# Attention with random features and a two-layer MLP on one core: the work of the first four pairs of heads, the key sums and the order of the instructions are changed

## The chip, the core and the metric

The kernel runs on one core of a Trainium2 chip. The engines that appear below are TensorE (PE in the rows; PEld is its weight load), VectorE (DVE), ScalarE (ACT), GpSimd (POOL) and SyncE (SP, which issues nearly all DMAs). The metric is device time in microseconds (us).

## The reference

There are 8 batches of 8 heads, 576 positions each, with a head dimension of 64 and 128 random features (`omega`). All data are float32.

```python
def phi(x):                                   # x is q or k, scaled by 64 ** -0.25
    proj = einsum('bhsd,md->bhsm', x, omega)
    h = proj - sum(x * x, -1) / 2             # the sum of squares of each row
    return exp(h - max(h, -1)) / sqrt(128)

kv = einsum('bhsm,bhsd->bhmd', k_p, v)
z = sum(k_p, axis=2)                          # the key sums
num = einsum('bhsm,bhmd->bhsd', q_p, kv)
den = einsum('bhsm,bhm->bhs', q_p, z) + 1e-06 # the denominators
x = (num / den) laid out as 4608 tokens x 512
out = silu(x @ w_in) @ w_out                  # w_in 512 x 2048, w_out 2048 x 512
```

## The kernel before, in words

The 64 heads are worked on as 32 pairs (`NWIN`); four pairs make a batch's 512 columns of `x`. Rows of a pair are held in nine blocks of 128 positions (`NC`), the middle one (`MID`) split between the two heads. For each pair n the stages are: loads of the transposed rows (`raw`) and of the plain rows (`nat`); the squares (`square`, L479, ACT) and their sums (`square_sum`, L488, DVE); projections (`project` L496, `project_mid` L502, PE, float32); row maxima (`top`, L509 and L511, DVE) and the bias made of maximum and square sum (`shift`, L517, DVE, tiles nbk and nbq); exponentials (`expo`, L534, ACT) into hk and hq. From hk come the key sums: for the first eight pairs (`DIRECT`) by PE alone (`zsum_direct`, L569 and L571), afterwards by four steps of additions on POOL (`sums`, L554 to L559) whose result `es`, 128x256, is summed over partitions by one float32 matmul against ones (`zsum`, L563). The denominators (`denom`) are nine blocks of products with the key sums, read from PSUM, each a fused multiply and add-up on DVE (L580) with a read of the accumulator, and then a reciprocal (L585). POOL scales hq by it (`normal`, L610), PE turns hq (`turn`, L616), ACT copies it out (`en_copy`, L628). `kv` (L592), its copies (`kt_copy` L597, `kw_copy` L605) and one turn (`kv_turn`, L600) prepare the right-hand factor of the numerators (`numer`, L654), whose result becomes `x` (`x_high` on ACT L673, `x_low` on DVE L678).

Meanwhile the weights are read, converted (`exponent` L738, `word` L752 to L758 on DVE) and split into a high and a low fp32r part (`weight_high` L771, `weight_low` L775 on POOL). The MLP of the first three batches runs as plain matmuls in three fp32r passes of 128x512 (L829 and L1075); the rest runs in two groups of block products with fewer multiplications (L914, L1028). Its matmuls lie between those of the attention on the same PE queue.

Nobody writes the order by hand: each step is a unit of a planner (`Plan`), with an engine, a due time (`key`), what it needs, the buffers it takes (`RINGS`, `HOMES`) and a cost (`COST`). `Plan.run` simulates the engines, and each engine executes its steps in the order so found. The due times are moved about by a table of seeds (`SHIFTS`). An engine that waits for one instruction holds back all that stand behind it.

## Time and profile before

| | |
|---|---|
| median of 3 runs (lowest to highest) | 1011.54 us (1010.02 to 1013.14) |
| the profiled execution | 1012.55 us |
| its span in the trace | 1010.4 us |
| PE busy | 982.1 us, 97% of the span |
| DVE busy | 760.1 us, 75% |
| ACT busy | 632.2 us, 63% |
| POOL busy | 367.4 us, 36% |
| mean granted clock of PE | 0.995 |

The span is counted from the first to the last instruction of the trace; 2.15 us of the profiled execution's time lie outside it. Busy shares are averages over stages that differ: the first 115 us are attention and weights, then attention and MLP are mixed, and from about 830 us on there is MLP alone. Ends of matmuls are modelled, so costs on PE are best read as the distance from the start of one group to the start of the next.

### The profile page before, as it was taken

Reading aid. Unit: us, or ns where it says so; the run is one execution under the profiler, and the core shown is the slowest. Engines: PE = TensorE matmul, PEld = TensorE weight load, DVE = VectorE, ACT = ScalarE, POOL = GpSimd, SP = SyncE. Lnnn points to the kernel's source line nnn. Section 1 sums busy time; section 2 is a strip of 40 time slices with the busy share of each in tenths; the row PEclk is TensorE's granted clock in tenths of the full one; section 3 lists DMA queues with packets and bytes.
Section 4 is the critical chain, followed back from the end, with each engine's and each line's share of the span. In section 5 each row is a group of like instructions: output and inputs, shape, how many; then the busy total and the mean of one; then the engine's idle time right before and its main releaser. Section 6 shows DMA issues by size and latency. Waiting matters only on the chain.

```text
span 1010.4 us, 17322 instructions
## 1 busy us (share of the span) xinstructions
PE 982.1 (97%) x5770; PEld 787.0 (78%) x5770; DVE 760.1 (75%) x1898; ACT 632.2 (63%) x1235; POOL 367.4 (36%) x447
## 2 busy tenths in 40 slices
PE   8799999999999999999999999999999999999997
PEld 7577877877777777777888777878887878888886
DVE  6988899876777677796666899995448977546962
ACT  6777776677656866676777775664858454334541
POOL 1455555777776775544642024120110100000000
PEclk9899999999999999999999999999999999999999
DMA  9667777787876976748986658875455677655665
GB/s 359 230 195 265 238 256 230 220 288 243 267 258 196 299 251 205 231 151 276 330 277 235 214 196 268 253 220 200 164 171 178 222 246 256 194 188 191 195 211 153
DMA packets 107592, 232.94 MB, mean 231 GB/s; under 512 B 14704, under 2 KB 39408, under 8 KB 107504
## 3 DMA queue, kind: packets, MB, share of 16 engines
q1 hardware_dynamic: 107200, 231.52, 69.8%
q8 instruction: 46, 0.75, 0.3%
q10 hardware_dynamic: 304, 0.33, 0.1%
q14 instruction: 42, 0.34, 0.1%
HBM read 182.52 MB, written 49.28 MB: 229 GB/s over the span
## 4 chain that ended last, share of the span: by engine, by line
PE 75%; DVE 15%; ACT 5%; DMA 3%; issue 2%; POOL 1%; DVEq 0%; ACTq 0%; POOLq 0%
PE ps_acc L914 18%; PE ps_acc L1028 12%; PE ps_acc L1075 10%; PE ps_h L829 7%; PE ps_att L496 4%; DVE prod L580 3%; PE ps_fx L829 2%; PE ps_att L1028 2%; PE ps_att L914 2%; PE ps_fx L1028 2%; PE ps_h L1028 2%; PE ps_fx L914 2%; PE ps_att L592 1%; PE ps_h L914 1%; DVE w L1018 1%
## 5 line engine op out<-in xcount | busy, mean ns | idle before, releaser
L914 PE MATMUL ps_acc<-w,x 128*128 128x512 f32 x792 | 189.7, 394 | 0.1
L610 POOL TENSOR_TENSOR hq<-hq,rd 128x384 f32<-128x384 f32 x96 | 91.0, 973 | 245.4 <-DVE rd L585 240.4
L914 PEld LDWEIGHTS ps_acc<-w,x 128*128 128x128 f32 x792 | 146.7, 188 | 32.4 <-DVE w L723 0.5
L1075 PE MATMUL ps_acc<-wo,gh 128*128 128x512 f32 x384 | 124.4, 405 | 0.0
L829 PE MATMUL ps_h<-x,w 128*128 128x512 f32 x432 | 116.7, 404 | 2.7 <-ACT gf L968 2.0
L1028 PE MATMUL ps_acc<-w,x 128*128 128x512 f32 x456 | 115.3, 394 | 0.0
L1028 PEld LDWEIGHTS ps_acc<-w,x 128*128 128x128 f32 x456 | 84.7, 188 | 18.8 <-DVE w L1018 0.4
L829 PEld LDWEIGHTS ps_h<-x,w 128*128 128x128 f32 x432 | 78.2, 189 | 21.4 <-issue 2.4
L580 DVE CUSTOM_DVE_ANT_0 prod<-hq,ps_att 128x128 f32<-128x128 f32 (+1 forms) x230 | 65.8, 286 | 22.2 <-ACT kw L605 8.6
L1075 PEld LDWEIGHTS ps_acc<-wo,gh 128*128 128x128 f32 x384 | 67.9, 188 | 14.4
L1028 PE MATMUL ps_acc<-gh,x 128*128 128x512 f32 x208 | 74.4, 396 | 1.4 <-DMA x<-wt 1.4
L1075 PE MATMUL ps_acc<-wo,gl 128*128 128x512 f32 x192 | 75.4, 393 | 0.0
L972 DVE TENSOR_TENSOR gl<-gf,gh 128x512 fp32r<-128x512 f32 x48 | 38.5, 802 | 24.9 <-ACT gf L968 24.6
L554 POOL TENSOR_TENSOR t<-hk 128x256 f32<-128x256 f32 x48 | 38.4, 820 | 36.2 <-ACT hk L548 24.8
L1028 PEld LDWEIGHTS ps_acc<-gh,x 128*128 128x128 f32 x208 | 39.0, 188 | 10.7 <-issue 1.8
L1075 PEld LDWEIGHTS ps_acc<-wo,gl 128*128 128x128 f32 x192 | 36.0, 188 | 8.1
L1028 PE MATMUL ps_acc<-gl,x 128*128 128x512 f32 x104 | 40.7, 391 | 0.0
L479 ACT ACTIVATE nat<-nat 128x576 f32<-128x576 f32 x58 | 40.0, 694 | 0.3 <-DMA nat<-kn 0.3
L628 ACT COPY en<-ps_att 128x384 f32<-128x384 f32 x45 | 21.2, 488 | 29.6 <-PE ps_att L616 24.8
L511 DVE TENSOR_REDUCE smk<-ps_att 128x4 f32<-128x512 f32 x42 | 27.7, 681 | 14.1 <-PE ps_att L496 10.1
L534 ACT ACT_TABLE_LOAD x24 | 30.8, 1283 | 12.0 <-DVE nbk L517 7.3
L829 PE MATMUL ps_fx<-x,w 128*128 128x512 f32 x144 | 37.8, 396 | 0.0
(434 smaller groups left out, 2379.8 us busy)
## 6 DMA issues: line engine op xcount, KB each, us to landing
x<-ws SPq DMA_DIRECT2D x84, 512.0 KB, 4.2
x<-wt SPq DMA_DIRECT2D x48, 512.0 KB, 4.2
x<-wo_d SPq DMA_DIRECT2D x72, 256.0 KB, 3.2
wo<-wo_d SPq DMA_DIRECT2D x32, 512.0 KB, 4.3
rawk<-kT SPq DMA_DIRECT2D x30, 352.0 KB, 4.3
rawq<-qT SPq DMA_DIRECT2D x30, 352.0 KB, 4.9
v<-v SPq DMA_DIRECT2D x30, 320.0 KB, 4.7
nat<-kn SPq DMA_DIRECT2D x29, 288.0 KB, 4.3
```

The source lines that it names most:

```text
L479: nc.scalar.activation(nat, nat, AF.Square, scale=SCALE * 0.5**0.5)
L496: nc.tensor.matmul(ps[:, i * M : (i + 1) * M], raw[r, o : o + P], oms[r], start=True, stop=True)
L511: nc.vector.tensor_reduce(m[:, 5 * j : 5 * j + 4], ps.rearrange("p (c m) -> p c m", m=M), AX.X, ALU.max)
L534: nc.scalar.activation(h[:, c], ps[:, i * M : (i + 1) * M], AF.Exp, bias=nb[:, c : c + 1])
L554: nc.gpsimd.tensor_tensor(t[:, j], e[:, 5 * j : 5 * j + 2], e[:, 5 * j + 2 : 5 * j + 4], ALU.add)
L580: nc.vector.tensor_tensor_reduce(out=prod[r], in0=e[r, c], in1=z[r, j * M : (j + 1) * M], scale=1.0, scalar=GUARD, op0=ALU.mult, op1=ALU.a ...
L610: nc.gpsimd.tensor_tensor(e[:, c], e[:, c], rd[:, c].unsqueeze(2).broadcast_to([P, 3, M]), ALU.mult)
L829: nc.tensor.matmul(ph, w[:, i], x[:, j], start=k == 0 and n == 0, stop=k == NK - 1 and n == 2)
L914: nc.tensor.matmul(ph, ws[:, u, kk * P : (kk + 1) * P], o[:, x], start=i in (0, 1, 4) and kk == 0 and n == 0, stop=kk == 1 and n == 2, ski ...
L972: nc.vector.tensor_tensor(gl, T.pop(("gf", t, f)), T["gh", t, f].bitcast(F32), ALU.subtract)
L1028: nc.tensor.matmul(T["qb", p, chain][d], w[:, u, d * P : (d + 1) * P], x, start=i in (0, 1, 4) and s == 0 and n == 0, stop=s == NS - 1 and ...
L1075: nc.tensor.matmul(T["po", t][j], g[:, js], w, start=f == 0 and n == 0, stop=f == NF - 1 and n == 2)
```

## The change

For the first four pairs (`SHARE`) the squares are made by POOL instead of ACT (the scale then becomes a small extra instruction on DVE), and the denominators by a copy of the key sums from PSUM to SBUF on ACT, products on POOL (two of 128x512, two of 64x128), and on DVE one reduction of 128x9x128, one small addition and the reciprocal. From the ninth pair on, POOL splits the key sums into a high and a low fp32r part (two more instructions of 128x256), and PE sums them in two fp32r passes instead of one float32 matmul; from the tenth on the turn of kv is no longer behind the key sums but behind the second group of turns of hq. The load of omega is issued by SP as its first DMA, no longer by ACT. A seventh warm-up matmul is added. The scratch tiles `prod` and `es` go; `zp` comes, and the products use a buffer of ring `en`. Costs, constants, the way of choosing among ready steps, and the whole table of seeds are other ones, so that the order on every engine is new.

```diff
-WARM = 6
+SHARE = 4
+WARM = 7
-    45253, 12939, 63401, 47171, 48605, 47566, 42730, 5774, 83395, 62489, 16880, 27634, 67040, 8136, 46225,
+    82336, 88449, 46253, 47699, 57731, 212, 16446, 12734, 86717, 29045, 39768, 53214, 56989, 74460, 88726,
...
     def load_omega():
-        nc.scalar.dma_start(omr, om_in)
+        nc.sync.dma_start(omr, om_in)
...
     def square(n, who):
         nat = T["nat", n, who]
+        if n < SHARE:
+            nc.gpsimd.tensor_tensor(nat, nat, nat, ALU.mult)
+            return
         nc.scalar.activation(nat, nat, AF.Square, scale=SCALE * 0.5**0.5)
...
+        if n < SHARE:
+            s = T["sm", n, who][:, 1, :NC]
+            nc.vector.tensor_scalar(s, s, SCALE * SCALE * 0.5, None, ALU.mult)
...
+    def sums_high(n):
+        T["zp", n] = zp = new("zp", [P, 2, 2, M], F32R)
+        nc.gpsimd.tensor_copy(zp[:, 0], T["es", n])
+
+    def sums_low(n):
+        zp = T["zp", n]
+        nc.gpsimd.tensor_tensor(zp[:, 1], T.pop(("es", n)), zp[:, 0].bitcast(F32), ALU.subtract)
 
     def zsum(n, ps):
-        es = T.pop(("es", n))
-        nc.tensor.matmul(ps[:, : 2 * M], ones, es.rearrange("p j m -> p (j m)"), start=True, stop=True)
+        zp = T.pop(("zp", n)).rearrange("p two j m -> p two (j m)")
+        for i in range(2):
+            nc.tensor.matmul(ps[:, : 2 * M], ones_r, zp[:, i], start=not i, stop=bool(i))
         T["z", n] = ps
...
+    def z_copy(n):
+        z, T["zs", n] = T.pop(("z", n)), new("t", [P, 2, M])
+        nc.scalar.copy(T["zs", n].rearrange("p j m -> p (j m)"), z[:, : 2 * M])
+
+    def weighted(n):
+        e, z = T["h", n, "q"], T.pop(("zs", n))
+        T["ez", n] = ez = new("en", [P, NC, M])
+        for j in range(2):
+            c, r = slice(5 * j, 5 * j + 4), slice(j * D, (j + 1) * D)
+            nc.gpsimd.tensor_tensor(ez[:, c], e[:, c], z[:, j : j + 1].broadcast_to([P, 4, M]), ALU.mult)
+            nc.gpsimd.tensor_tensor(ez[r, MID], e[r, MID], z[r, j], ALU.mult)
+
     def denom(n):
+        if n < SHARE:
+            den = new("den", [P, NC])
+            nc.vector.tensor_reduce(den, T.pop(("ez", n)), AX.X, ALU.add)
+            nc.vector.tensor_scalar(den, den, GUARD, None, ALU.add)
+            T["rd", n] = rd = new("rd", [P, NC])
+            nc.vector.reciprocal(rd, den)
+            return
...
         T["t", n, g] = ps[:, off : off + 3 * P]
+        if n > DIRECT and g == 1:
+            kv_turn(n, ps, 3 * P)
...
-    def zsum_turn(n, ps):
-        zsum(n, ps)
-        kv_turn(n, ps, 2 * M)
```

On POOL, at the start of the program, there stood no work of the attention before the first pair's scaling of hq (`hq<-hq,rd`); `w_475` and the like are homes of MLP weights:

```order
L443 MEMSET sides 64x128 x2
L610 TENSOR_TENSOR hq<-hq,rd 128x384 x3
L771 CAST w_475<-w_445 128x512
L775 TENSOR_TENSOR w_475<-w_445,w_475 128x512
L610 TENSOR_TENSOR hq<-hq,rd 128x384 x3
```

Now squares (`nat`, and `w_191` to `w_268`, which hold plain rows of the pairs 1 to 3) and products (`en<-hq,t`) stand there:

```order
L498 TENSOR_TENSOR nat<-nat 128x576 x2
L498 TENSOR_TENSOR w_191<-w_191 128x576
L498 TENSOR_TENSOR w_207<-w_207 128x576
L617 TENSOR_TENSOR en<-hq,t 128x512
L618 TENSOR_TENSOR en<-hq,t 64x128
L617 TENSOR_TENSOR en<-hq,t 128x512
L618 TENSOR_TENSOR en<-hq,t 64x128
L498 TENSOR_TENSOR w_224<-w_224 128x576
L498 TENSOR_TENSOR w_227<-w_227 128x576
L663 TENSOR_TENSOR hq<-hq,rd 128x384 x3
```

The first scaling is now behind six squares and four products.

On DVE, the end of the first pair's denominators (ten products, the last two shown) stood ahead of all work on the second pair's queries (smq, nbq):

```order
L580 ISA prod,den<-hq,ps_att 128x128
L580 ISA den 128x1
L585 RECIPROCAL rd<-den 128x9
L511 TENSOR_REDUCE smq<-ps_acc 128x4
L488 TENSOR_REDUCE smq<-w_193 128x9
L511 TENSOR_REDUCE smq<-ps_acc 128x4
L509 TENSOR_REDUCE smq<-ps_acc 128x1
L517 TENSOR_REDUCE smq<-smq 128x9
L517 TENSOR_REDUCE nbq<-smq 128x9
```

Now the second pair's key bias (nbk) and the first half of its query maxima stand ahead of the reduction of POOL's products (`den<-en`), and the rest of them behind it:

```order
L541 TENSOR_REDUCE nbk<-smk 128x9
L535 TENSOR_REDUCE smq<-ps_acc 128x4
L623 TENSOR_REDUCE den<-en 128x9
L624 TENSOR_SCALAR den<-den 128x9
L626 RECIPROCAL rd<-den 128x9
L533 TENSOR_REDUCE smq<-ps_acc 128x1
L535 TENSOR_REDUCE smq<-ps_acc 128x4
L541 TENSOR_REDUCE smq<-smq 128x9
L541 TENSOR_REDUCE nbq<-smq 128x9
```

Twenty-one instructions have become three in front of the second pair's query bias, and the first of the three reads what POOL has made.

On PE, at the eleventh pair, the key sums and the turn of kv stood between passes of the MLP (L829), three passes behind the numerators (L654):

```order
L592 MATMUL ps_fx<-hk,v 64x128 x10
L654 MATMUL ps_att<-en,kw 64x512 x2
L654 MATMUL ps_fx<-en,kw 64x64 x2
L829 MATMUL ps_h<-x_1943,w_1210 128x512 x3
L563 MATMUL ps_att<-es,ones 128x256
L600 MATMUL ps_att<-ident,kt 128x128
L829 MATMUL ps_h<-x_2267,w_1210 128x512 x3
```

Now nine passes (L880, L1126) lie between the numerators (L705) and the key sums, and the turn of kv follows turns of hq:

```order
L705 MATMUL ps_att<-en,kw 64x64 x2
L880 MATMUL ps_fx<-x_1612,w_1258 128x512 x3
L1126 MATMUL ps_acc<-wo,gh 128x512 x2
L1126 MATMUL ps_acc<-wo,gl 128x512
L1126 MATMUL ps_acc<-wo,gh 128x512 x2
L1126 MATMUL ps_acc<-wo,gl 128x512
L597 MATMUL ps_att<-zp,ones_r 128x256 x2
L1126 MATMUL ps_acc<-wo,gh 128x512 x2
...
L669 MATMUL ps_fx<-ident,hq 128x128 x3
L669 MATMUL ps_att<-ident,hq 128x128 x3
L653 MATMUL ps_att<-ident,kt 128x128
L1126 MATMUL ps_acc<-wo,gh 128x512 x2
```

The key sums have moved back behind other passes, and no float32 matmul stands with them any more.

Over the whole program, PE goes from float32 matmuls or turns to fp32r passes and back in 303 places before, and in 269 now.

## Rows read from the trace of the kernel before

**Rows 1.** The page: busy time by engine, and the granted clock in 40 slices.

```profile
PE 982.1 (97%) x5770; PEld 787.0 (78%) x5770; DVE 760.1 (75%) x1898; ACT 632.2 (63%) x1235; POOL 367.4 (36%) x447
...
PEclk9899999999999999999999999999999999999999
```

**Rows 2.** Busy time by stretch: length, PE, PEld, DVE, ACT, POOL, clock, DMA, GB/s.

```profile
20.00:70.00 50.00, 39.88 (x343) 32.50 (x345) 45.35 (x158) 35.65 (x107) 23.05 (x25) 0.90 0.71 242
70.00:115.00 45.00, 42.51 (x246) 33.05 (x243) 39.96 (x83) 34.01 (x70) 25.42 (x24) 1.00 0.71 237
200.00:500.00 300.00, 298.42 (x1964) 234.88 (x1963) 216.82 (x672) 202.35 (x357) 199.48 (x260) 1.00 0.77 249
500.00:1010.40 510.40, 500.57 (x2565) 405.03 (x2563) 371.55 (x776) 288.85 (x559) 65.25 (x80) 1.00 0.65 212
```

**Rows 3.** Waits of PE, 0 to 75 us: total, times, longest.

```profile
PE ps_att L496 <- DVE den L580: 2.9, 1, 2.9
PE ps_fx L616 <- issue: 2.6, 1, 2.6
PE ps_acc L616 <- POOL hq L610: 1.8, 2, 1.0
```

**Rows 4.** Timeline of PE at a key sum: start, length.

```profile
218.49 0.86 PE L829 MATMUL ps_h<-x,w 128*128 128x512 f32 x3
219.19 0.59 PE L563 MATMUL ps_att<-es,ones 128*128 128x256 f32 x2
219.65 0.71 PE L1075 MATMUL ps_acc<-wo,gh 128*128 128x512 f32 x2
220.20 0.40 PE L1075 MATMUL ps_acc<-wo,gl 128*128 128x512 f32 x1
```

**Rows 5.** Timeline of PE at turns of hq.

```profile
284.76 0.49 PE L616 MATMUL ps_fx<-ident,hq 128*128 128x128 f32 x3
285.09 0.49 PE L616 MATMUL ps_att<-ident,hq 128*128 128x128 f32 x3
```

**Rows 6.** Groups of DVE, 0 to 70 us: count, busy us, mean ns, idle before.

```profile
L580 DVE CUSTOM_DVE_ANT_0 prod<-hq,ps_att 128x128 f32<-128x128 f32 x24 | 6.9, 286 | 2.3 <-PE ps_att L571 0.8
L580 DVE DVE_READ_ACCUMULATOR2_ANT den<- 128x1 f32 x40 | 3.3, 82 | 0.0
L488 DVE TENSOR_REDUCE smk<-nat 128x9 f32<-128x576 f32 x4 | 3.0, 744 | 0.0
L517 DVE TENSOR_REDUCE smk<-smk 128x9 f32<-128x18 f32 x4 | 0.7, 174 | 0.1
```

**Rows 7.** Groups of ACT, 0 to 70 us.

```profile
L479 ACT ACTIVATE nat<-nat 128x576 f32<-128x576 f32 x9 | 6.4, 709 | 0.3 <-DMA nat<-kn 0.3
L628 ACT COPY en<-ps_acc 128x384 f32<-128x384 f32 x8 | 4.0, 509 | 0.4 <-PE ps_acc L616 0.4
```

**Rows 8.** Single lines of POOL and DVE: duration ns least/median/most, first and last start.

```profile
L610 POOL TENSOR_TENSOR hq<-hq,rd x96: 819/830/1338, 20.2 to 806.7; 128x384 f32<-128x384 f32 x96
...
L775 POOL TENSOR_TENSOR wo<-w,wo x16: 1263/1293/1769, 42.7 to 192.4; 128x512 fp32r<-128x512 f32 x16
...
L771 POOL CAST wo<-w x16: 599/612/950, 42.0 to 191.7; 128x512 fp32r<-128x512 f32 x16
...
L559 POOL TENSOR_TENSOR es<-es,hk x48: 446/456/950, 182.5 to 758.1; 64x128 f32<-64x128 f32 x48
...
L556 POOL TENSOR_TENSOR es<-t x24: 723/736/1065, 181.7 to 751.8; 128x256 f32<-128x256 f32 x24
...
L754 DVE SCALAR_TENSOR_TENSOR w<-wre,w x32: 630/692/1797, 24.1 to 190.1; 128x512 uint32<-128x512 uint32 x32
```

**Rows 9.** Timeline of POOL and PE where the key sums are latest.

```profile
253.18 0.97 POOL L559 TENSOR_TENSOR es<-es,hk 64x128 f32<-64x128 f32 x2
...
254.26 0.64 PE L563 MATMUL ps_fx<-es,ones 128*128 128x256 f32 x2
```

**Rows 10.** Timeline of PE at the start.

```profile
4.64 2.08 PE L496 MATMUL ps_att<-oms,rawk 64*128 64x128 f32 x16 [0.65 <-ACT oms L461]
```

More of the change, by code (lines that the diff above doesn't have):

```diff
@@ L75 @@
 SLOW = 8.332
-MLP_STEP = 2.725
-PRO = 18.575
+MLP_STEP = 2.721
+PRO = 17.988
 SWITCH = 1.42
-STAY = 22.527
+STAY = 19.181
 HANDOFF = {"PE": 0.053, "ACT": 0.034, "DVE": 0.034, "POOL": 0.075, "SP": 0.08}
-CALM = 0.127
-JOIN = -0.001
+CALM = 0.114
+JOIN = 0.0
+WAIT_PE = 0.25
+WAIT_ACT = 0.25
+WAIT_DVE = 0.25
+WAIT_POOL = 0.25
+HASTE = 0.0
 AGAIN = 0.03
-EASE = -0.003
+READY = {"PE": 1.06, "ACT": 2.5, "DVE": 1.0, "POOL": 2.2, "SP": 0.75}
+COLD = 7.0
+EASE = 0.0
 FORMS = {"s1": 0, "s2": 0, "m": 0, "m2": 0, "proj": 2, "kv": 3, "num": 3, "kvnum": 3}
@@ L255, in add @@
         u["occ"], u["took"] = self.cost(u)
-        u["form"] = FORMS.get(kind, 1) if eng == "PE" else 0
-        u["moved"] = (MOVED.get(kind, 0.74) if eng == "SP" else 0.4) if lat else 0.0
+        u["form"] = 0 if kind == "z" and name[1] >= DIRECT else FORMS.get(kind, 1) if eng == "PE" else 0
+        u["moved"] = MOVED.get(kind, 0.74) if lat and eng == "SP" else 0.4 if lat else 0.0
         for i in free:
@@ L276, in cost @@
             return (0.27, 0.35) if n[3] == 2 else (0.605, 0.69)
+        if kind == "den" and n[1] < SHARE:
+            return 1.45, 1.5
+        if kind == "ssum" and n[1] < SHARE:
+            return 0.76, 0.85
+        if kind == "sq" and n[1] < SHARE:
+            return 0.8, 0.85
         if kind == "wd" and n[-1] == 0:
             return 0.34, 0.42
+        if kind == "turn" and n[1] > DIRECT and n[2] == 1:
+            return 0.434, 0.6
         if kind in COST:
@@ L286, in run @@
         end = {}
-        port, warm = 0.0, 0.0
+        port, warm = 0.0, COLD
         read = {}
@@ L290, in run @@
         pipe = 0.0
-        free_at = {e: 0.0 for e in ("PE", "ACT", "DVE", "POOL", "SP")}
-        table, form, resume = None, 1, 0.0
+        free_at = dict(READY)
+        table, form, resume = "exp", 1, 0.0
+        wait = {"PE": WAIT_PE, "ACT": WAIT_ACT, "DVE": WAIT_DVE, "POOL": WAIT_POOL, "SP": 0.25}
         order = []
@@ L369, in run @@
                 least = min(p[3] for p in picks)
-                p = min((p for p in picks if p[3] <= least + 0.25), key=lambda p: p[2:])
+                p = min((p for p in picks if p[3] <= least + wait[e]), key=lambda p: (p[2] + HASTE * (p[3] - least), p[3]))
                 if best is None or p[3] < best[3]:
@@ L437, in attention_mlp @@
     nc.vector.memset(ones, 1.0)
+    ones_r = const.tile([P, P], F32R, tag="ones_r", name="ones_r")
+    nc.vector.tensor_copy(ones_r, ones)
     omr = const.tile([P, M], F32, tag="omr", name="omr")
@@ L1199, in attention_mlp @@
         if n > DIRECT:
-            kx = zn
+            kx = ("turn", n, 1)
         else:
```

64 lines of the change are left out of this document (36 added, 28 removed), and 78 rows, old and new, of tables (RINGS, SHIFTS).

## The prediction

> **What bounds the kernel now.** I read the page's busy times first. PE is busy for 97% of the span at nearly the full clock, DVE for 75%, ACT for 63%, POOL for 36% [rows 1]. So a microsecond of PE work that goes is worth a microsecond almost everywhere; the other engines count only where PE waits for them. The second view, busy time by stretch, says where that is. Between 200 and 500 us PE lacks 300.0 - 298.4 = 1.6 us, and from 500 us to the end 9.8 us, part of which is the last output's way out. Between 20 and 70 us it lacks 50.0 - 39.9 = 10.1 us, and its mean clock is 0.90 there: granted 1.2 instead of 2.4 GHz for about a tenth of the time, which is some 5 us at half speed and costs about 2.5 us of work, at the lower level after idle time. Between 70 and 115 us it lacks 2.5 us [rows 2]. In the stretch of 20 to 70 us DVE is busy for 45.4 of 50 us, ACT for 35.7 and POOL for 23.1: DVE is the engine that limits there [rows 2]. The third view, PE's waits in that time, names single places: 2.9 us for DVE's denominators at a projection, 2.6 us at a turn, 1.8 us for POOL's scaling [rows 3]. By the kernel's text the projection does not read denominators: it needs a PSUM bank, and those products read the key sums from one.
>
> **Key sums on PE, pairs 9 to 32 (24 of them).** In the timeline the float32 key sum begins at 219.19 and the next passes at 219.65, with the turn of kv in these 0.46 us. The first two passes after it take 220.20 - 219.65 = 0.55 us. Three passes of the MLP ahead take 219.19 - 218.49 = 0.70, so two take 0.47, and the return from float32 costs 0.08 more [rows 4]. Before: 0.54 us. Now: two passes of 256 columns at 0.70 / 3 for 512 columns make 0.23 us without a change of form, and the turn of kv in a group of turns costs what another turn does, (285.09 - 284.76) / 3 = 0.11 us [rows 5]. The gain is 0.54 - 0.34 = 0.20 us a pair, times 24: 4.8 us. No row shows an fp32r pass of 256 columns. If it took as long as one of 512, 0.23 us each, the gain would be -0.03 us a pair, so about -1 us in all; if the passes were free, it would be 10 us. I take 4.8, since the many passes of 512 are the same form at twice the length. The 34 fewer changes of form are not counted again: about as many vanish as key sums stood alone between passes.
>
> **What POOL needs for that.** The split adds a cast and a subtraction of 128x256. Half the cast of 128x512 is 0.31 us and the addition of 128x256 takes 0.74 [rows 8]: 1.05 us more between key sums and PE. In the tightest place POOL ended at 253.18 + 0.97 = 254.15 and PE began at 254.26 [rows 9], so there the old place would come a microsecond too early. What then waits is PE's queue: the passes of the MLP behind it, and behind the sums DVE's denominators. At the eleventh pair three passes of the MLP stood between the numerators and the key sums, and now nine do, six passes or 6 x 0.23 = 1.4 us more cover; so I cost it at 0. Without cover it is 1.05 us in each of the 24 places, 25 us; with work in front it is nothing, or below nothing if the new place also fits other waits better, by no more than the 1.6 us that PE lacks between 200 and 500 us [rows 2].
>
> **Denominators and squares of the first four pairs.** Ten products of 0.286 us and ten reads of 0.082 make 3.7 us of DVE, with the reciprocal, as long as another small instruction at 0.17, 3.9 [rows 6]. Now: one reduction of 9x128 = 1152 values; that of 576 takes 0.744 [rows 6], so 1.49, and two small ones of 0.17: 1.8 us. Eight scalings of the square sums come, 8 x 0.17 = 1.4. DVE is relieved of 4 x (3.9 - 1.8) - 1.4 = 7.0 us. ACT loses eight squares of 0.71 and gets four copies of 128x256, at most 0.51 each as for 128x384 [rows 7]: relieved of 3.6 us or more. POOL gets eight squares of 576: between the cast's rate, 0.612 x 576 / 512 = 0.69 us, and the subtraction's, 1.293 x 576 / 512 = 1.45; I take 1.45, a form with two inputs: 11.6 us. The products per pair are two of 128x512, between 0.830 x 512 / 384 = 1.11 (the scaling, also with a broadcast factor) and 1.29, and two of 64x128 at 0.46 [rows 8]: 3.1 to 3.5 us, 13 us in all. POOL so goes from 23 to about 47 us of the 50 from 20 to 70 us [rows 2] at the worst, less what falls before 20 us (the first squares) or behind 70.
>
> The path of one pair becomes longer. From the end of the exponentials it was 3.9 us on DVE; now it is 0.5 us on ACT, 3.3 on POOL, 1.8 on DVE: 5.6, so 1.7 us more. In return DVE can do the next pair's maxima while POOL multiplies, and the bank with the key sums is free after ACT's copy, not after the tenth product; the wait of 2.9 us should vanish. What is late next are PE's turns, which wait for POOL's scaling behind the squares in its queue. DVE's wait at the reduction is new: behind it stands the rest of the second pair's query maxima and bias, for which ACT's exponentials wait.
>
> What of it reaches the end? The most is all of DVE's 7.0 us with 2.5 us of cold clock, 9.5; the least is a loss of four times 1.7, 6.8 us. DVE is full to nine tenths in the stretch, so I take the relief of DVE less the longer path of one pair, the last, since the other three overlap: 7.0 - 1.7 = 5.3 us, and of it three quarters, 4 us, because PE's own work of 39.9 us in 50 and the transfers are in part next in line.
>
> **The rest.** Omega first: PE's first projection waited 0.65 us for it [rows 10]; the key rows come behind it in SP's queue now, so between 0.65 gained and as much lost; 0. The seventh warm-up stands in PE's wait for omega: 0, or 0.2 us if that wait is gone. The new order elsewhere: PE lacks 9.8 us from 500 us on [rows 2]; an order can win some 3 of them or lose as many; 0.
>
> **Sum.** The profiled execution took 1012.55 us, its span and 2.15 us around it, 1.0 above the median of 1011.54. 1012.55 - 4.8 - 4 = 1003.75; on the scale of the median 1002.7. I say 1003.
>
> **Rivals**, on the scale of the median.
> 1. *The relief is eaten by a common port.* DVE's combination of weight words took 0.69 us at the median and 1.80 at most [rows 8]: something holds it at times, though no row says what. If POOL does, and if each of DVE's two-input instructions in the stretch, some twenty, were held for half of a 1.3 us POOL instruction at a share of a half, it would be 20 x 0.65 x 0.5 = 6.5 us, nearly the relief of 7.0. Left are the key sums: 1011.5 - 4.8 = 1006.7. Against it: the reductions, the bulk of DVE's work there, stay at 0.744. The Trainium skill, "Perfetto Trace Analysis", section "Optimizing Scalar/DVE Operations", says that the two engines share a read port, "so offloading operations between those two might not help". The trace agrees so far as the 1.80 goes.
> 2. *Slower: the longer path sets the end of the head.* If each pair's denominators are waited for on the way to the next pair's (DVE stands at the reduction, the query bias behind it), the path grows by 1.7 us at my prices and by 2.9 at the longest spans (1.34 for a scaling of 384, so 1.78 for a product of 512 [rows 8]) in each of four pairs, and DVE's relief is idle time. With the squares in POOL's queue ahead of products and scaling, another 1.45 a pair: 4 x (2.9 + 1.45) = 17.4, less 4.8: 1024; in the milder form 4 x (1.7 + 1.45) - 4.8 = 7.8: 1019. It decides from 1.2 us lost a pair on, where it eats the key sums' 4.8. For it: four waits of this kind would stand on the one place where PE has no MLP work yet. Against it: in the new order the second pair's key bias and half of its query maxima stand ahead of DVE's wait.
> 3. *No gain: PE waits for the split.* If a quarter of the 24 places lack cover, 6 x 1.05 = 6.3 us, and the head gives 2: 1011.5 - 4.8 + 6.3 - 2 = 1011.
> 4. *More: both long waits and the cold clock go.* 2.9 + 2.6 [rows 3] + 2.5 of clock, with 4.8: 1011.5 - 12.8 = 998.7.
>
> **How the numbers follow.** The forecast, a gain of 6 to 12 us, has 0.48; rival 1 0.17; rival 2 0.11; rival 3 0.12; rival 4 0.12. The range of 8 in 10 leaves out the far half of rival 4 and rival 2: 994 to 1012. The forecast's own is 999.5 to 1005.5. A measurement of this kernel tells about 0.3% (3 us) from no change, so faster is below 1008.5: forecast, rival 4, and most of rival 1: 0.74. Within 0.3%: rival 3 and the rest of rival 1, 0.14. Slower: rival 2 and a little of rival 3, 0.12.
>
> **What would show it.** Key sums: their two passes start 0.11 to 0.12 us apart and the passes behind them come without the 0.08; PE's busy time is some 5 us less. Head: PE's lack between 20 and 70 us falls from 10 to about 6, the 2.9 us wait for a bank is gone, DVE is below 9 tenths. Wrong would be: waits of DVE for POOL's products of over 1 us in several pairs (rival 2), two-input instructions of DVE with a median above 0.9 us in the first 70 us (rival 1), or waits of PE at key sums (rival 3).

## The result, and the profile after

The changed kernel takes 1018.8 us (median of 5 runs, 1016.15 to 1020.26) against 1013.14 us for the kernel before beside it: a ratio of 1.0059, with an interval of 1.0035 to 1.0084. It is slower, by about 6 us; the forecast was 1003 us, 8 to 9 faster. The profiled execution took 1019.93 us, with a span of 1018.1.

The page of the kernel after, busy times and granted clock (before: [rows 1]):

```profile
PE 988.2 (97%) x5774; PEld 789.0 (77%) x5774; DVE 756.5 (74%) x1835; ACT 642.6 (63%) x1241; POOL 417.7 (41%) x519
...
PEclk8799999999999999999999999999999999999999
```

PE is busy 6 us *longer*, though the key sums took work from it: the first two slices of the clock are lower, and matmuls last longer at the lower clock. Below, the head means the first 115 us, in which the first pairs are worked on and the plain MLP passes begin. Busy time by stretch (columns as in [rows 2], and the first 20 us):

```profile
0.00:20.00 20.00, 16.41 (x135) 14.63 (x137) 9.95 (x26) 9.54 (x33) 8.59 (x16) 0.83 0.92 333
20.00:70.00 50.00, 40.35 (x315) 30.38 (x312) 40.57 (x82) 31.67 (x99) 31.61 (x36) 0.83 0.55 190
70.00:115.00 45.00, 40.88 (x263) 32.22 (x262) 40.49 (x99) 34.33 (x72) 27.24 (x27) 1.00 0.73 258
200.00:500.00 300.00, 299.50 (x1959) 236.67 (x1958) 217.74 (x689) 217.37 (x365) 213.14 (x285) 1.00 0.76 248
500.00:1018.10 518.10, 506.17 (x2591) 407.18 (x2589) 371.38 (x775) 292.52 (x567) 83.33 (x108) 0.99 0.65 212
```

Between 20 and 70 us VectorE's busy time did fall, from 45.4 to 40.6 us, and ScalarE's from 35.7 to 31.7; GpSimd's rose from 23.1 to 31.6, all in the direction foreseen. But PE's idle time there stayed (9.7 us for 10.1) and its clock went from 0.90 to 0.83. In the first 20 us PE is idle for 3.6 us at 0.83 (before 2.1 at 1.00), between 70 and 115 us for 4.1 instead of 2.5. VectorE's busy time fell, and nothing came of it. The waits of PE up to 75 us show what took the places of those in [rows 3] (us in total, times, longest):

```profile
PE ps_h L669 <- ACT hk L558: 2.1, 1, 2.1
PE ps_acc L705 <- ACT en L679: 1.9, 1, 1.9
PE ps_fx L669 <- ACT hk L558: 1.7, 2, 1.2
PE ps_acc L520 <- DMA rawq<-qT: 1.6, 1, 1.6
PE ps_acc L669 <- POOL hq L663: 1.3, 2, 1.1
```

The 2.9 us wait for a PSUM bank is gone, as predicted. Now PE waits for ScalarE, and ScalarE in turn for VectorE's bias of the keys: first the row of the kernel after, then that of before, both for the first 80 us. Of the 15.4 us the longest wait, 8.2, is at the very start, where ScalarE used to make the squares; the other three, 7.2 us, compare with the 4.4 of before.

```profile
ACT hk L558 <- DVE nbk L541: 15.4, 4, 8.2
```

```profile
ACT hk L534 <- DVE nbk L517: 4.4, 2, 3.0
```

Why a relieved VectorE delivers its bias later is seen in its queue. The second pair's query bias and the first pair's denominators (start, length):

```profile
19.13 0.69 DVE L535 TENSOR_REDUCE smq<-ps_acc 128x4 f32<-128x512 f32 x1 [2.14 <-PE ps_acc L520]
20.72 1.35 DVE L623 TENSOR_REDUCE den<-en 128x9 f32<-128x1152 f32 x1 [0.90 <-POOL en L618]
22.11 0.94 DVE L624 TENSOR_SCALAR den<-den 128x9 f32<-128x9 f32 x1
23.08 0.21 DVE L626 RECIPROCAL rd<-den 128x9 f32<-128x9 f32 x1
...
24.28 0.17 DVE L541 TENSOR_REDUCE nbq<-smq 128x9 f32<-128x18 f32 x1
```

The queue stands for 0.90 us before the reduction; the small addition takes 0.94; and the query bias, for which ScalarE waits, comes at 24.28 instead of at 22.22 before. The copy of the key sums began at 16.80, the reciprocal ended at 23.30: 6.5 us, in the other three pairs 7.5, 6.2 and 8.9. Before, the four denominators ended 3.6 to 4.3 us after their first product began.

The chain of work that ended last, followed back from its end, runs through this step in each of the first four pairs, as it did through the denominators of three of them before. In the second pair it runs from the reduction to the third pair's key bias and to ScalarE's exponentials (start, length):

```profile
34.80 1.27 DVE den L623
...
36.91 0.18 DVE nbk L541
37.11 2.18 ACT hk L558 x8
```

The third pair's key bias comes at 36.91 instead of 32.51. In the third pair the chain takes in the whole step, from ScalarE's copy on:

```profile
47.98 0.37 ACT t L610
48.42 1.28 POOL en L617
...
51.88 1.36 DVE den L623
...
54.55 0.18 DVE nbk L541
54.82 1.14 ACT hk L558 x4
```

The key sums on PE (start, length), to be held against [rows 4]:

```profile
217.84 0.39 PE L597 MATMUL ps_att<-zp,ones_r 128*128 128x256 f32 x2
218.07 0.63 PE L1126 MATMUL ps_acc<-wo,gh 128*128 128x512 f32 x2
218.54 0.39 PE L1126 MATMUL ps_acc<-wo,gl 128*128 128x512 f32 x1
```

Two passes take 218.07 - 217.84 = 0.23 us, and the two passes behind them 218.54 - 218.07 = 0.47, so without the 0.08 of a return: exactly the forecast.

And two stretches of 3.4 us at 1.2 GHz are new far behind the head, at 592 and 616 us, each behind a wait of PE of 2.0 and 1.7 us. The kernel before has none between 55 and 1010 us.

### The profile page after: what moved, and what is told of

The parts are those of the page before. It is cut to its first block, busy times and chain, and to the rows that moved or that the text cites. A ratio compares the mean times of both kernels' runs of the same rounds, so it can differ in the third digit from the quotient of the medians.

```text
span 1018.1 us, 17347 instructions
## 1 busy us (share of the span) xinstructions
PE 988.2 (97%) x5774; PEld 789.0 (77%) x5774; DVE 756.5 (74%) x1835; ACT 642.6 (63%) x1241; POOL 417.7 (41%) x519
## 4 chain that ended last, share of the span: by engine, by line
PE 82%; DVE 11%; ACT 2%; DMA 2%; POOL 1%; issue 1%; SPq 0%; DVEq 0%; POOLq 0%; ACTq 0%
PE ps_acc L965 18%; PE ps_acc L1126 12%; PE ps_acc L1079 11%; PE ps_h L880 9%; PE ps_fx L880 4%; PE ps_att L1079 3%; PE ps_att L520 3%; PE ps_att L645 2%; PE ps_fx L965 2%; PE ps_att L965 2%; PE ps_att L669 2%; DVE w L1069 2%; PE ps_att L705 2%; PE ps_fx L520 1%; PE ps_h L965 1%; DVE omr L633 1%
## 5 line engine op out<-in xcount | busy, mean ns | idle before, releaser
L663 POOL TENSOR_TENSOR hq<-hq,rd 128x384 f32<-128x384 f32 x96 | 85.0, 909 | 172.4 <-DVE rd L638 152.8
L1126 PE MATMUL ps_acc<-wo,gh 128*128 128x512 f32 x384 | 123.0, 401 | 0.0
L880 PE MATMUL ps_h<-x,w 128*128 128x512 f32 x420 | 113.0, 402 | 2.6 <-ACT hk L558 1.2
L880 PEld LDWEIGHTS ps_h<-x,w 128*128 128x128 f32 x420 | 75.7, 188 | 20.2 <-ACT x L724 1.5
L1126 PEld LDWEIGHTS ps_acc<-wo,gh 128*128 128x128 f32 x384 | 68.5, 188 | 13.4
L1126 PE MATMUL ps_acc<-wo,gl 128*128 128x512 f32 x192 | 75.2, 392 | 0.0
L633 DVE CUSTOM_DVE_ANT_0 omr<-hq,ps_att 128x128 f32<-128x128 f32 (+1 forms) x180 | 51.5, 286 | 19.1 <-PE ps_att L597 10.7
L1126 PEld LDWEIGHTS ps_acc<-wo,gl 128*128 128x128 f32 x192 | 36.0, 188 | 8.0
L679 ACT COPY en<-ps_att 128x384 f32<-128x384 f32 x59 | 28.4, 489 | 20.7 <-PE ps_att L669 14.3
L880 PE MATMUL ps_fx<-x,w 128*128 128x512 f32 x156 | 41.0, 400 | 0.0
L535 DVE TENSOR_REDUCE smk<-ps_att 128x4 f32<-128x512 f32 x43 | 28.3, 685 | 12.4 <-PE ps_att L520 11.3
```

Source lines behind the costliest of these rows:

```text
L633: nc.vector.tensor_tensor_reduce(out=prod[r], in0=e[r, c], in1=z[r, j * M : (j + 1) * M], scale=1.0, scalar=GUARD, op0=ALU.mult, op1=ALU.a ...
L663: nc.gpsimd.tensor_tensor(e[:, c], e[:, c], rd[:, c].unsqueeze(2).broadcast_to([P, 3, M]), ALU.mult)
L679: nc.scalar.copy(T["en", n][:, 3 * g * P : 3 * (g + 1) * P], T.pop(("t", n, g)))
L880: nc.tensor.matmul(ph, w[:, i], x[:, j], start=k == 0 and n == 0, stop=k == NK - 1 and n == 2)
L1126: nc.tensor.matmul(T["po", t][j], g[:, js], w, start=f == 0 and n == 0, stop=f == NF - 1 and n == 2)
```

## The experiments

Ratios are to the kernel before on the same chip, with a 95% interval from 5 rounds. Where a kernel has the instruction order of another one, "lag" is the difference in start of the same PE instruction in the two traces.

### Parts of the change in the order of before

Key sums alone (the two fp32r passes and GpSimd's two instructions, in all 24 pairs; as in the change, the sums stay in the buffer of their terms):

```diff
-        nc.tensor.matmul(ps[:, : 2 * M], ones, es..., start=True, stop=True)
+        for i in range(2):
+            nc.tensor.matmul(ps[:, : 2 * M], ones_r, zp[:, i], start=not i, stop=bool(i))
```

> The kernel before with its own order, and one part of the change alone: from the ninth pair on the key sums are split by GpSimd and summed in two fp32r passes; the turn of kv stays behind them. If the term of the sum is right (0.20 us a pair, of which 0.1 needs the turn moved away), this is 3 to 5 us faster than before. If an fp32r pass of 256 columns costs like one of 512, it is the same as before; if the split makes TensorE wait in many of the 24 places, it is slower.

1014.18 us, 1.0026 (1.0015 to 1.0038): slower. Key sum and turn of kv do take 0.263 instead of 0.458 us on PE, 0.195 less in each pair. It is lost again in single places: 1.3 us near 260 us where PE now waits for GpSimd's split, 2.3 between 670 and 683 us with a stretch of 3.4 us at 1.2 GHz from 682 on, 0.5 to 1.2 in five others. (The traced execution took 1016.88 us, 2.7 above the median, so these places show more loss than the median has.) VectorE's subtraction of two SBUF operands in the MLP went from 801 to 858 ns in the mean between 200 and 500 us; its reductions stayed at 744.

Squares and denominators on GpSimd, both and each alone, and omega's load alone:

```diff
+            nc.gpsimd.tensor_tensor(nat, nat, nat, ALU.mult)              # squares, first four pairs
...
+                nc.gpsimd.tensor_tensor(ez[:, c], e[:, c], zs[...]..., ALU.mult)   # products
+            nc.vector.tensor_reduce(den, ez, AX.X, ALU.add)
...
-        nc.scalar.dma_start(omr, om_in)
+        nc.sync.dma_start(omr, om_in)
```

> The kernel before with its own order, and the squares and denominators of the first four pairs made with GpSimd, as in the change, at the places where they stood. Theory of the path: each pair's denominators come 2 to 3 us later on the way to its turns, so this is 4 to 10 us slower than before, with the fourth pair's numerators later than 69.7 us by as much. Theory of the clock and the order alone: the relief of VectorE and ScalarE makes it equal or up to 4 us faster.

> The kernel before with its own order; only the squares of the first four pairs are made by GpSimd, with their small scaling on VectorE. A square takes 1.12 us there in the trace of the changed kernel against 0.70 on ScalarE, but ScalarE is relieved of eight. If the loss of 12.7 us of the run with both edits comes from the denominators' path alone, this is within 1 us of the kernel before; if the squares in GpSimd's queue hold up the scaling, it is 3 us or more slower.

> The kernel before with its own order; only the denominators of the first four pairs are made by copy, products on GpSimd and reduction. From the copy to the reciprocal it took 5.7 to 7.3 us in the run with both edits, against 3.6 to 4.3 in the kernel before. Theory of the path: 8 to 12 us slower, all lost before 92 us. Theory of the clock: the loss follows the time at half speed, half of about 17 us more, and is not tied to the denominators.

> The kernel before with one edit: omega is loaded by SP's first DMA instead of ScalarE's queue. In the changed kernel the first projection began at 5.33 us instead of 4.64, waiting for the first keys. If the place in SP's queue is the reason, it begins some 0.5 us later here too and the whole is 0 to 1 us slower; if not, nothing changes.

Both: 1022.54 us, 1.0113 (1.0092 to 1.0134). Squares: 1013.97, 1.0020 (1.0012 to 1.0029). Denominators: 1019.13, 1.0069 (1.0053 to 1.0084). Omega: 1012.35, 0.9998 (0.9988 to 1.0008). The lag of the denominators' kernel is 2.8 us at 28 us, 5.8 at 51, 9.6 at 77, and then 9.1 to 8.7 to the end: it is made in three steps in the first four pairs, and later work gives back less than a microsecond of it. Its VectorE queue at the third step:

```profile
67.84 0.16 DVE L518 TENSOR_REDUCE nbq<-smq 128x1 f32<-128x2 f32 x1
72.01 1.36 DVE L586 TENSOR_REDUCE den<-en 128x9 f32<-128x1152 f32 x1 [4.00 <-POOL en L584]
```

and all its waits of this kind up to 80 us:

```profile
DVE den L586 <- POOL en L584: 16.1, 4, 4.7
```

VectorE stands for 16.1 us in four places, with work of the next pairs behind. So in this order moving the products off the busiest engine leaves it idle in their place. The squares' kernel lags by 2.6 us from 115 us on, the one with both by 12.4.

### The mechanism of the denominators

The same kernel, but GpSimd makes the products of one half of the heads, VectorE those of the other at the same time:

```diff
-                nc.gpsimd.tensor_tensor(ez[:, c], ...)
+                eng = nc.vector if j else nc.gpsimd
+                eng.tensor_tensor(ez[:, c], ...)
```

> The order of before; in the first four pairs the denominators go the new way (z copied by ScalarE, products, reduction), but GpSimd makes the products of one half of the heads and VectorE those of the other at the same time. In the trace of the experiment with all products on GpSimd, 1.28 + 0.45 + 1.27 + 0.45 = 3.4 us of products lie between the copy and the reduction and VectorE stands 4.0 us in front of the reduction; here 1.7 us of GpSimd are left, 0.75 + 0.25 of VectorE beside them. Theory (the step's length and VectorE's standing in front of it are the loss): of the 6.9 thousandths (7 us) of that experiment 4 pairs x 1.7 us = 6.8 come back: 1012 to 1015 us, ratio 1.000 to 1.003. Rival (GpSimd slows VectorE's operations, and VectorE's load is what counts): no less than 1.006, since the same number of operations run beside GpSimd and VectorE has 4 us more to do.

1016.14 us, 1.0043 (1.0031 to 1.0056): 3 us of 7 came back; the lag is 3.9 at the end instead of 8.7. The theory had 7, the rival none. What is left is the step itself, which is still longer than before. Its length in the four pairs, from the first product (before) or from the copy of the key sums to the end of the reciprocal, in us:

| kernel | first | second | third | fourth | longer than before, in all | lag behind the four pairs |
|---|---|---|---|---|---|---|
| before | 4.3 | 3.6 | 3.6 | 3.9 | | |
| order of before, denominators on GpSimd | 5.8 | 5.8 | 6.3 | 5.8 | 8.5 | 8.9 to 9.1 |
| order of before, products halved | 4.7 | 4.6 | 5.3 | 4.7 | 3.9 | 3.3 to 3.9 |
| order of before, squares and denominators | 5.7 | 7.3 | 6.2 | 5.9 | 9.8 | 12.4 |
| changed kernel | 6.5 | 7.5 | 6.2 | 8.9 | 13.7 | another order |
| changed kernel, products halved | 5.2 | 9.3 | 6.8 | 8.3 | 14.3 | another order |

In the order of before the lag is, within the scatter of the head, what the four steps grew by: 8.5 us for 8.9 to 9.1, 3.9 for 3.3 to 3.9, and with the squares' 2.6 us 9.8 + 2.6 = 12.4 for 12.4. (The scatter is 0.5 to 2 us: omega's load alone lags by 0.6 at 115 us, and the key sums of ten pairs, none of them in the head, by -1.9.) That is the path paid four times over. Why the halved step did not become as short as before is seen in the second pair on VectorE and GpSimd:

```profile
27.52 0.69 DVE L584 TENSOR_TENSOR en<-hq,t 128x512 f32<-128x512 f32 x1 [0.17 <-ACT t L579]
28.22 1.27 DVE L585 TENSOR_TENSOR en<-hq,t 64x128 f32<-64x128 f32 x1
29.84 1.35 DVE L587 TENSOR_REDUCE den<-en 128x9 f32<-128x1152 f32 x1 [0.35 <-POOL en L585]
```

```profile
27.57 1.78 POOL L584 TENSOR_TENSOR en<-hq,t 128x512 f32<-128x512 f32 x1 [0.70 <-ACT t L579]
29.30 0.50 POOL L585 TENSOR_TENSOR en<-hq,t 64x128 f32<-64x128 f32 x1
```

Each holds up the other: GpSimd's product takes 1.78 us instead of 1.27, and VectorE's product of 128 columns 1.27, longer than its own one of 512 columns in front. It ends at 29.49, just after GpSimd's at 29.35. So part of what the halving should have saved goes on the common way of the two engines to SBUF. The Trainium skill, "SBUF — State Buffer", section "SBUF: two separate sides", says that whoever comes first holds the shared ports for its whole instruction and that the other fully blocks. These rows agree with it.

The dummy matmuls of the kernel before taken out:

```diff
-HOT = 100.0
+HOT = 0.0
```

> The kernel before without the 3 + 4 dummy matmuls that stand ahead of the first pair's query projection and the second's key projection; the order is the same. It leaves PE idle there for some 1.7 us more, as the changed kernel is. Theory (idle time early in the head is paid twice, once as idle and once as a stretch at the clock's lower level): a new stretch at 1.2 GHz of 6.8 us at about 8 us into the span, as in the changed kernel, and 2 to 4 us longer, 1014 to 1016. Rival (the head's end is set by the pairs' chain on ScalarE, VectorE and GpSimd, which a slow PE does not hold up): the stretch appears but the end moves by less than 1 us, 1012 to 1013.

1013.4 us, 1.0005 (0.9996 to 1.0014), lag 0.5 us at 100 us and 1.0 at the end. The stretch at 8 us did not appear (the clock of the first 20 us stayed at 1.00); the one near 50 us grew from 3.4 to 6.8 us. The rival was nearer, since 3.4 us more at the lower level moved the head's end by half a microsecond: while the pairs' chain is late, a slow PE costs little. The changed kernel runs 23.9 us of its first 70 at 1.2 GHz (before: 10.2). By this run that is for the most part a sign of the lateness and not its cause, and the next experiment agrees; neither shows it for the whole 13.7 us.

### Parts of the change undone in the new order

Six dummy matmuls ahead of the first pair's query projection, where PE waits 1.6 us for a transfer:

```diff
+HEAT = {("proj", 0, "q"): 6}
```

> The changed kernel with one edit: six dummy matmuls on TensorE in front of the first pair's query projection, where it stood idle for 1.6 us for the query rows and where the kernel before had three. Theory of the clock: the stretch of 6.8 us at half speed that began at 8.1 us goes away, the second pair's key projection is some 3 us earlier, and the whole is 2 to 4 us faster than the changed kernel. Theory of the path: the head waits for GpSimd and VectorE anyway, and the gain is below 1 us.

1019.04 us, 1.0069 (1.0054 to 1.0084), not to be told from the changed kernel. The low stretch at 8 us went, and the two at 29 and 39 us became one of 17.1 us from 26 us on: 20.5 us of the first 70 at 1.2 GHz in place of 23.9.

The old squares and denominators in the new order; half of the products on VectorE in the new order; one float32 key sum again in the new order (the last leaves out the second of GpSimd's two instructions):

```diff
-        if n < SHARE:
+        if POOL_SQUARES and n < SHARE:        # False; for the denominators likewise
...
+            eng = nc.vector if j else nc.gpsimd
...
-            nc.tensor.matmul(ps[:, : 2 * M], ones_r, zp[:, i], start=not i, stop=bool(i))
+        nc.tensor.matmul(ps[:, : 2 * M], ones, zp, start=True, stop=True)
```

> The changed kernel with its own order, its key sums and its omega, but squares on ScalarE and denominators on VectorE as before. Theory of the path: the loss of the head (some 9 us up to 115 us) goes away for the most part and the key sums' 4 us stay, so 1008 to 1012 us, faster than or equal to the kernel before. If the new order is itself the cause, it stays at 1016 us or above.

> The changed kernel with the same halving in its own order: in the first four pairs VectorE makes the products of one half ahead of its reduction, GpSimd those of the other. Theory (the step from the copy of z to the reciprocal, 6.2 to 8.9 us there, sets the head): 1.7 us less a pair, 3 to 6 us faster than the changed kernel, 1013 to 1016 us. Rival (its head is set by the order, not by the step): within 1 us of the changed kernel, or slower where VectorE starts its products before other work that it was to do meanwhile, 1018 to 1021.

> The changed kernel's own order, pools and GpSimd head; only the key sums from the ninth pair on go back to one fp32 matmul (the second copy on GpSimd, which makes the fp32r rest, is left out; a plain copy of the sums stays). Theory (in an order that was made for it the fp32r key sum keeps its 0.195 us a pair, 24 x 0.195 = 4.7, and gives little of it back): 4 to 5 us slower than the changed kernel, 1023 us or a ratio of 1.010 to the kernel before. Rival (the split costs as much beside it, in VectorE's slowed two-input operations and in waits, as it saves, as it did in the order of before, where all 24 pairs gave 1.0026): within 1 us of the changed kernel, 1018.8 us or 1.006.

Old head: 1022.59 us, 1.0097 (1.0082 to 1.0112). Halved products: 1020.01, 1.0080 (1.0065 to 1.0094). Float32 key sums: 1019.91, 1.0077 (1.0064 to 1.0091). The first two theories miss: the new order is no place for the old head, and it gains nothing from the halving. With the old head each step takes 3.5 to 3.8 us again, and yet the fourth pair's numerators begin at 83.4 us (changed kernel 80.5, before 69.6): the new order alone, with the old steps, holds the head at least as late. So these runs can't say how much of the changed kernel's 11 us there is the steps' and how much the order's. The halving, in that order, did not shorten the steps (29.1 us in all without it, 29.6 with it), so its result speaks neither for nor against the step. The rival's reason, that VectorE's share of the products then stands in front of work that it used to do meanwhile, is not shown. The trace agrees with it: VectorE no longer waits at any of the four reductions, where it waited 2.1 us in all, and the steps still don't get shorter. The third has a lag of 1.6 us at 97 us and of 4.1 at 582, so the fp32r key sums earn 2.5 us in between; at 620 us it is 0.1. There the changed kernel has its two low stretches (first three rows, clock in the third column from the right), the float32 one has none (next three):

```profile
588.00:596.00 8.00, 6.01 (x50) 4.25 (x49) 7.90 (x15) 3.99 (x10) 1.59 (x2) 0.79 0.54 164
612.00:616.00 4.00, 1.83 (x13) 1.14 (x10) 4.00 (x6) 2.70 (x5) 3.42 (x4) 0.96 0.43 174
616.00:620.00 4.00, 4.00 (x13) 3.14 (x12) 3.93 (x9) 2.08 (x8) 0.00 (x0) 0.61 0.00 0
```

```profile
588.00:596.00 8.00, 7.01 (x62) 5.74 (x62) 7.83 (x17) 6.99 (x20) 3.27 (x4) 1.00 0.78 240
612.00:616.00 4.00, 2.50 (x34) 1.99 (x33) 4.00 (x5) 2.86 (x8) 3.78 (x5) 1.00 0.83 309
616.00:620.00 4.00, 3.30 (x14) 2.74 (x15) 3.93 (x9) 0.95 (x4) 0.10 (x1) 1.00 0.02 9
```

Near 590 us PE came 4.1 us earlier to work that ScalarE delivered only 3.1 us earlier, and waited 2.0 us instead of 1.0; then its clock fell. Near 614 us both kernels wait 0.5 and 1.7 us, and only the changed kernel's clock falls. The traces with the six dummy matmuls and with the halved products, which have the same order and key sums, show both low stretches again. That with the old head waits 1.9 us at the first place and its clock stays up; it has the second stretch alone. So the fall goes with the waits, but no single wait decides it in these traces, and what does is open.

Orders planned anew, once with the planner's prices for the new steps set to the measured ones, once with no pair on the new steps:

```diff
-            return 1.45, 1.5
+            return 1.85, 1.9
...
-    "ez": (2.0, 2.05)
+    "ez": (3.45, 3.5)
```

```diff
-SHARE = 4
+SHARE = 0
```

> The changed kernel with the planner's four prices for the new steps raised to what the trace after shows: squares 0.8 to 1.12 us, products with the key sums 2.0 to 3.45, the reduction with its two small operations 1.45 to 1.85, the square's sum with its scaling 0.76 to 1.15; the order is planned anew from them. Theory A (the order was built on prices that were too low, so PE stands waiting in places where the planner saw none): 3 to 6 us faster than the changed kernel, 1013 to 1016 us. Theory B (no order helps, since the pair's chain itself has become longer by the products): within 2 us of it, 1017 to 1021. A planner's order also moves by some us with any change of its prices, so a difference under 3 us proves neither.

> The changed kernel with no pair on GpSimd's new steps (squares on ScalarE, denominators on VectorE as in the kernel before), planned anew with that; key sums in two fp32r passes and the omega load first stay. It is the experiment with the old head in the new order, but with an order made for the old head. Theory (the GpSimd steps of the first four pairs are the loss, the rest is worth its 4 us): 1008 us, ratio 0.996, and time to the fifth numerator's start about 92 us as before. Rival (the new numbers of the planner are themselves bad in the head, whoever does the squares and denominators; the old head in the new order gave 1.0097): 1018 us or more.

1027.71 us, 1.0147 (1.0131 to 1.0163), and 1038.31, 1.0266 (1.0252 to 1.0280): both theories miss. The table of seeds belongs to one set of prices; with these two others the order is a new draw and worse by 9 and 20 us. But the repriced order shows that the new steps need not hold the head by 11 us: in it they are 11.0 us longer than before in all, and yet the fourth pair's numerators begin at 71.5 us (before 69.6), and PE is idle for 13.5 us up to 115 us (before 14.7). It loses its time behind that, first with 7.9 us of idle PE from 115 to 200 us (before 2.2). So it stays open whether a well-chosen order for the new steps would be faster; these two runs don't answer it.

### Where the key sums' saving goes

The order of before, fp32r key sums in eleven pairs only; the same with five dummy matmuls at the place of its loss; the same without pair 20:

```diff
+SPLIT = (8, 9, 12, 13, 14, 15, 18, 19, 20, 23, 24)
...
+HEAT = {("turn", 20, 1): 5}
...
+SPLIT = (8, 9, 12, 13, 14, 15, 18, 19, 23, 24)
```

> The kernel before with its own order and fp32r key sums in 11 pairs only: those in which TensorE came to the key sums over 1.7 us after GpSimd had ended them, and before 560 us, where VectorE is not yet full. 11 x 0.2 = 2.2 us faster if the loss of the run with all 24 came from the tight places and from the full stretch of VectorE; slower by about 1 us if splitting costs everywhere.

> The kernel with fp32r key sums in eleven pairs in the order of before, and 5 dummy matmuls ahead of the transposes of pair 20 where PE waited 1.8 us at 446 us and then ran at 1.2 GHz for 3.4 us. Theory (that low stretch, not a slower VectorE, took the key sums' gain): no low stretch there, the time difference to before stays at -1.7 us beyond 455 us and reaches 11 x 0.195 = 2.1 us at the end: ratio 0.998. Rival (the wait and what follows come from VectorE and return in another form): 1.000 again.

> The order of before with the key sums of ten pairs in two fp32r passes, as in the experiment with eleven, but pair 20 as before. Theory (the extra work for pair 20 on GpSimd and VectorE's slower operations beside it make the wait at 446 us that bit longer, and the clock falls): no low stretch at 446 us, the difference to before goes on falling by 0.195 us a pair, 10 x 0.195 = 2.0 us in all: 1010.1 us where before has 1012.1, ratio 0.998. Rival (each pair's saving is lost at some other wait): ratio 1.000, and the trace shows another place where 1 to 2 us go.

Eleven pairs: 1011.72 us, 1.0000 (0.9988 to 1.0012). The lag falls by 0.9 us up to 444 us, half of what nine pairs save, since some of the 0.2 us steps are lost again at the next wait; then it jumps by 2.25 before 455. With dummies: 1012.77, 1.0012 (1.0001 to 1.0023). Without pair 20: 1010.72 us beside 1012.22, 0.9991 (0.9981 to 1.0001), the best version of this study, though the interval includes 1. The 4 us from 444 us on, in this order (before last):

```profile
444.00:448.00 4.00, 2.20 (x8) 1.57 (x8) 3.76 (x11) 1.08 (x3) 2.63 (x3) 0.78 0.34 90
```

```profile
444.00:448.00 4.00, 1.88 (x12) 1.29 (x11) 3.83 (x8) 0.86 (x2) 3.66 (x4) 1.00 0.27 90
```

```profile
444.00:448.00 4.00, 2.89 (x17) 2.58 (x18) 3.78 (x11) 2.31 (x3) 1.26 (x2) 1.00 0.36 92
```

```profile
444.00:448.00 4.00, 2.45 (x15) 1.88 (x14) 3.83 (x9) 0.80 (x3) 3.57 (x4) 1.00 0.29 90
```

Before, PE waited 1.6 us here for a bank that VectorE frees, at the full clock. With pair 20 split it waited 1.8 and the clock fell; without, 1.5, and the lag goes on falling, from -1.4 at 97 us (the head's own scatter, as nothing is changed there) to -2.3 at 444 and -2.6 at 547. The dummies missed their aim: they need the same bank, so they stood behind the wait and added 1.2 us; with the 0.7 us that PE came earlier and waited longer for it and for GpSimd, these are the 1.9 lost there. That the clock stayed up in that run can't be put down to them.

## Why the prediction was wrong

**The step that failed** is "What of it reaches the end?": "DVE is full to nine tenths in the stretch, so I take the relief of DVE less the longer path of one pair, the last, since the other three overlap". The head was taken as a matter of VectorE's load, and the longer path was charged once. (The chain that ended last in the kernel before, which already runs through the denominators in three of the four pairs, would have been the view to ask.) VectorE's busy time between 20 and 70 us fell by 4.8 us and PE's idle time did not. In the order of before, the other three did not overlap: the denominators' step grew by 1.5 to 2.8 us in each of the four pairs, 8.5 us in all, and the lag behind them is 8.9. In the changed kernel the chain that ended last runs through the step, or its part on VectorE, in all four pairs. What sets the head is a chain through PE, VectorE, ScalarE and GpSimd in which each pair's denominators stand in VectorE's in-order queue ahead of the next pairs' bias.

**What stays open** is how much of the changed kernel's own loss this is. Its fourth pair's numerators begin 11 us later than before; its steps are 13.7 us longer; but with the old steps in its order they begin 14 us later, and with the new steps in the repriced order 2. The prediction asked what the new order elsewhere could win or lose, and put it at 0; that the order of the head might itself lose was no term of its sum.

**The longer path was also mis-sized**: 5.6 us were predicted, and it took 6.2 to 8.9. Most single prices were near: copy 0.37 to 0.51 (0.5 predicted), products 1.27 and 0.45 twice, 3.4 (3.3), reduction 1.35 (1.49), reciprocal 0.21. The small addition was put at 0.17, and took 0.94, 0.17, 0.64 and 0.82; the rest is waiting between the engines. Squares were taken at 1.45 and took 1.15, so GpSimd was dearer on paper than in fact, and its busy time between 20 and 70 us rose to 31.6 us, not to 47; the squares' loss in the order of before is 2 to 3 us.

**The relief was mis-sized too**: 7.0 us were priced, and about 2.8 are left. Before, the four denominators held VectorE for 15.3 us (15.6 priced). Now reduction, addition and reciprocal hold it for 9.1 (7.3 priced) and the eight scalings of the square sums take 3.4 (1.4 priced). That the stretch from 20 to 70 us fell by 4.8 us is in part a matter of which work falls into it: over the whole span VectorE's busy time fell by 3.6.

**Rival 2 comes nearest**: "DVE stands at the reduction, the query bias behind it", with 1019 us in its milder form. That the number fits is luck in part: the rival kept the key sums' 4.8 us and took 1.7 us for the longer path, where the key sums brought next to nothing and the step grew by 2.2 to 5.0 us a pair. The argument against it, that the new order puts other work in front, holds for half: in the new order VectorE stands for 2.1 us in all there, in the old one for 16.1. But in it the first pair's key bias stands behind GpSimd's square (10.82 us instead of 9.79), the second pair's query bias behind the reduction, and the third pair's key bias behind the second reduction.

**The key sums** were right in size (0.195 us a pair for 0.20), and wrong in what arrives: of 4.7 us the trace of the changed kernel keeps 2.5 up to 582 us and gives them back at two places with a falling clock. "So a microsecond of PE work that goes is worth a microsecond almost everywhere" overlooks that PE then comes sooner to a delivery that does not come as much sooner. Rival 3 (waits for the split) was seen clearly only in the old order, in 1 of 24 places. The cover counted for the new order was there for the most part: in two of its 24 places, at 437 and 456 us, the second pass starts 0.38 and 0.49 us behind the first instead of 0.12, some 0.6 us in all, of which the list of waits shows 0.2.

**Rival 1** (the common port) is real in another place than the one it named: two-input instructions of weights had a mean of 0.69 and 0.73 us in the first 80 us, below the 0.9 named as its mark. It was the small ones that were held. The four additions and eight scalings took 6.0 us where 2.1 were priced, and these 3.9 us are more than half of the relief of 7.0.

**The clock's price was halved**: a mean of 0.90 over 50 us, at two levels of which one is half, means a fifth of the time at 1.2 GHz and not a tenth, 10 us and 5 us of work instead of "some 5 us" and "about 2.5". It enters only rival 4 and the upper bound of the head.

**Right**: omega's load at 0 (ratio 0.9998 alone), the wait for the bank gone, the direction of GpSimd's rise, and PE's idle time from 500 us on within the 3 us allowed (9.8 before; 518.1 - 506.2 = 11.9). The seventh warm-up was not tried alone; in the changed kernel the first projection begins at 5.33 us instead of 4.64, behind a wait of 0.9 us for the key rows, where omega's load alone gave 4.73.

The account on the scale of the traces: the spans differ by 7.7 us, 1.6 of them idle time of PE and 6.1 busy time. Idle time grew by 2.6 us up to 115 us, shrank by 3.2 from there to 500 us, and grew by 2.1 behind. Busy time: 13.7 us more at half speed in the head are worth at most 6.8 of work, the two late stretches 3.4, and the key sums take 4.7 off in full; that makes 5.5 at most, and 0.6 or more has no place in this account. How the head's part divides between squares, denominators and order in the new order is open, since no experiment there could change one and keep the others.

## What to carry to other kernels

An engine's load in a stretch says what could be won, not what limits: before work is moved off a busy engine, follow the next stage's inputs back through that engine's queue and count what stands behind the instruction that will now wait. A step split over three engines is paid once per iteration when its last part sits in an in-order queue ahead of the next iteration's first. When the order is changed together with the steps, an experiment that undoes the steps alone no longer tells what they cost. And on an engine that is busy for 97%, a small saving arrives only where the engines that feed it are ahead too: here 0.2 us less work ahead of a wait was often 0.2 us more wait, and behind some of these waits stood 3.4 us at 1.2 GHz, worth 1.7.

## What the hardware showed beside

The addition on 9 values a partition, and the scaling of the square sums likewise, in the changed kernel (ns least/median/most):

```profile
L624 DVE TENSOR_SCALAR den<-den x4: 173/730/935, 22.1 to 74.6; 128x9 f32<-128x9 f32 x4
```

```profile
L512 DVE TENSOR_SCALAR smq<-smq x4: 171/294/1235, 10.2 to 30.7; 128x9 f32<-128x9 f32 x4
```

One of them began at 30.66 us, beside a product that GpSimd had begun at 30.60 and that took 1.27 us, and lasted 1.24: as long as what was left of GpSimd's instruction. Reductions of 576 values beside the same work stayed at 0.74, and small reductions at 0.17. The Trainium skill, "GPSIMD Engine Reference", section "Specifications", names as the contending instructions of VectorE those with two SBUF inputs or in a mode that uses both ports. The trace agrees so far that some of VectorE's instructions are held and others not. Among those held is a nine-value instruction of one input; whether it runs in such a mode, no row says. The size of the instruction is no protection.

The square of 128x576 with the same operand twice took 1.146 us on GpSimd, every one of eight within 4 ns, though a subtraction of 128x512 with two operands takes 1.27.
